# A planned attention and token/channel mixing kernel: transposes and loads expected to land later, and a larger stock of channel work

## The chip, the cores and the metric

One core of a Trainium2 chip. The time is the device time of one execution in microseconds (us). Most comparisons are of several timed runs of a kernel against runs of the kernel before on the same chip in the same rounds; a ratio is the mean time of one kernel's fast runs over the mean of the other's fast runs of those rounds, so it is not quite the ratio of the medians that stand beside it. A run counts as slow when it lies over 1.5% above the fastest of its kernel. On one core that is only a mark of length, and one of the findings below is what makes such runs long.

## The reference

Batch 8, 12 heads, sequence 448, head size 64. Attention without softmax, then a token mixer and a channel mixer:

```python
scores = q @ k.T / sqrt(64);  attn = maximum(scores, 0)**2 / 448;  x = attn @ v     # heads merged: [8, 448, 768]
h = maximum(x.T @ w_tok1, 0) @ w_tok2;  u = x + h.T                                 # w_tok1 [448, 256], w_tok2 [256, 448]
out = u + maximum(u @ w_ch1, 0) @ w_ch2                                             # w_ch1 [768, 1536], w_ch2 [1536, 768]
```

## The kernel before

The work is cut into 24 groups of four heads (three groups make a batch). Per group: 7 scores `S`, values `V`, a crossbar transpose of the attention output `xd` (from group 6 on), two token steps `t1` and `t2`. Per batch: 12 first channel steps `C1` and six or eight second ones `C2` (14 for a pair of batches). Keys and queries are transposed by TensorE up to group 8 and by a crossbar transfer `kd` from group 9 on, which reads from one interleave buffer `kqi` that VectorE or ScalarE fills.

Nothing of this runs in the order of the source. A planner in the kernel's own Python plays the program through with assumed durations and decides in which order each engine gets its instructions. On the chip that order is fixed; each engine waits at the head of its list (in the profile of before VectorE stood 4.17 us at one copy, and the scores behind it waited 1.60 us for its next eviction).

```python
class Planner:
    def run(self, todo, reserve, least, lanes=8):
        ...
                if o.work is not None:                       # a DMA: when does the planner expect it to land?
                    ring = max(ring, t + o.dur + 1.2) + o.work
                    o.seen = ring + 1.0 + SEM
                    landed[e].append(o.seen)
        ...
                    # o is attention work (scores, values): how much channel work is owed before the next?
                        over = sum(v for k, v in rest.items() if k < b) - reserve[min(b, len(reserve) - 1)]
                        owed += max(least, over / n)
...
    RES, LEAST = (0.0, 18.0, 10.0), 0.4
...
            xback[s] = add(Op(f"xd{s}", "SP", <crossbar transpose x_sb <- xT>, xe[s] + [old], dur=1.23, work=2.0))
            ready = xback[s]                                 # t1 waits for it
```

`rest` is the channel work of batches whose attention is done. What lies above `reserve` is spread between the attention work; what lies below is kept in hand, as filler for when attention has to wait.

## Time and profile before

| | before |
|---|---|
| timed runs first seen | 383.7 us median of 3 (383.02 to 388.58) |
| profiled execution | 382.1 us, span 380.2 |
| TensorE (PE) busy | 358.9 us of the span |
| TensorE idle: start, 40 to 280 us, tail | 5.1, 11.5, 4.7 us |
| crossbar transposes of x: landing min, median, max | 3.0, 6.0, 10.4 us |

In the profile's tables of stretches, the first figure after the stretch is its length, the next the time in which TensorE was busy, then weight loads, VectorE, ScalarE and GpSimd, the granted TensorE clock, the DMA share and GB/s. A line `A <- B: x, n, y` in the waits says that A waited for B x us in total, n times, y at the longest. The chain that ended last, by engine, of the kernel before:

```profile
PE 74%; DMA 17%; DVE 3%; ACT 3%; issue 2%; POOL 0%; ACTq 0%; DVEq 0%; POOLq 0%
```

17% of the path that set the end was spent in DMA: that is the share to watch.

### The profile page before, as it was taken

Reading aid. Unit: us, or ns where it says so; the run is one execution under the profiler, and the core shown is the slowest. Engines: PE = TensorE matmul, PEld = TensorE weight load, DVE = VectorE, ACT = ScalarE, POOL = GpSimd, SP = SyncE. Lnnn points to the kernel's source line nnn. Section 1 sums busy time; section 2 is a strip of 40 time slices with the busy share of each in tenths; the row PEclk is TensorE's granted clock in tenths of the full one; section 3 lists DMA queues with packets and bytes.
Section 4 is the critical chain, followed back from the end, with each engine's and each line's share of the span. In section 5 each row is a group of like instructions: output and inputs, shape, how many; then the busy total and the mean of one; then the engine's idle time right before and its main releaser. Section 6 shows DMA issues by size and latency. Waiting matters only on the chain.

```text
span 380.2 us, 8633 instructions
## 1 busy us (share of the span) xinstructions
PE 358.9 (94%) x3441; PEld 193.5 (51%) x3441; DVE 221.1 (58%) x406; ACT 210.5 (55%) x431; POOL 93.2 (25%) x159
## 2 busy tenths in 40 slices
PE   7998999999989999996998979999899999999995
PEld 3454555655455554543554534555446555565562
DVE  2999548764647774774265764568455785432021
ACT  3999858357646686265444465635662567512400
POOL 8992152840303330240033032031210000000000
PEclk9999999999999999999999998999999999999999
DMA  7999999999699999599199996996944641234023
GB/s 97 181 184 164 182 207 198 190 187 166 97 164 158 178 192 129 76 187 189 36 105 145 195 141 87 162 166 156 158 74 96 108 101 38 43 84 112 0 75 92
DMA packets 99352, 50.38 MB, mean 133 GB/s; under 512 B 72752, under 2 KB 95728, under 8 KB 99312
## 3 DMA queue, kind: packets, MB, share of 16 engines
q0 software_dynamic: 25424, 21.70, 42.8%
q1 hardware_dynamic: 73808, 27.93, 41.9%
q8 instruction: 27, 0.44, 0.5%
q14 instruction: 13, 0.11, 0.1%
q10 hardware_dynamic: 80, 0.20, 0.1%
HBM read 43.38 MB, written 11.01 MB: 143 GB/s over the span
## 4 chain that ended last, share of the span: by engine, by line
PE 74%; DMA 17%; DVE 3%; ACT 3%; issue 2%; POOL 0%; ACTq 0%; DVEq 0%; POOLq 0%
PE m_ps L762 24%; PE m_ps L729 23%; DMA x_sb<-xT 13%; PE acc_ps L538 8%; PE sc_ps L487 8%; PE t_ps L645 5%; PE h_ps L673 4%; DMA kqT<-kqi 3%; ACT sq L277 2%; DVE sq L520 1%; DMA q_raw<-in_q_dram 1%; PE kqT_ps L440 1%; ACT r_sb L277 1%; DVE kqT L285 0%; ACT kqT L283 0%
## 5 line engine op out<-in xcount | busy, mean ns | idle before, releaser
L277 ACT ACTIVATE sq<-sc_ps 128x448 bf16<-128x448 f32 x270 | 125.6, 571 | 40.0 <-PE sc_ps L487 40.0
L729 PE MATMUL m_ps<-uT_sb,wc 128*128 128x448 bf16 x576 | 116.2, 355 | 0.0
L762 PE MATMUL m_ps<-wc,r_sb 128*128 128x384 bf16 x672 | 114.1, 326 | 0.0
L520 DVE TENSOR_TENSOR sq<-sq 128x896 bf16<-128x896 bf16 x168 | 97.7, 618 | 6.4 <-ACT sq L277 6.2
L762 PEld LDWEIGHTS <-r_sb 128*128 128x128 bf16 x672 | 64.7, 98 | 45.3 <-issue 3.9
L729 PEld LDWEIGHTS <-wc 128*128 128x128 bf16 x576 | 55.4, 98 | 53.6 <-issue 5.8
L277 ACT ACTIVATE r_sb<-m_ps 128x448 bf16<-128x448 f32 x95 | 52.7, 556 | 48.4 <-PE m_ps L729 48.1
L300 POOL DMA_DIRECT2D v_raw<-in_v_dram x48 | 28.9, 611 | 169.6 <-PE sc_ps L487 159.2
L775 DVE TENSOR_TENSOR out_sb<-m_ps,u_sb 128x384 f32<-128x384 f32 x56 | 31.1, 556 | 61.1 <-PE m_ps L762 61.1
L279 DVE TENSOR_SCALAR sq<-sc_ps 128x448 bf16<-128x448 f32 x66 | 39.4, 619 | 43.6 <-PE sc_ps L487 43.6
L487 PE MATMUL sc_ps<-kqT 64*64 64x448 bf16 x672 | 52.9, 372 | 3.8 <-DVE out_sb L775 1.6
L538 PE MATMUL acc_ps<-sq,v_raw 64*64 64x448 bf16 x672 | 37.3, 356 | 0.0
L685 DVE TENSOR_TENSOR uT_sb<-h_ps,xT 128x448 bf16<-128x448 f32 x48 | 27.6, 617 | 12.7 <-PE h_ps L673 12.7
L645 PE MATMUL t_ps<-x_sb,wt 128*128 128x256 bf16 x192 | 25.7, 278 | 9.0 <-DMA x_sb<-xT 8.3
L487 PEld LDWEIGHTS <-kqT 64*64 64x64 bf16 x672 | 18.9, 107 | 28.5 <-issue 21.5
L277 ACT ACTIVATE r_sb<-t_ps 128x512 bf16<-128x512 f32 x24 | 14.8, 616 | 30.6 <-PE t_ps L645 30.3
L300 POOL DMA_DIRECT2D q_raw<-in_q_dram x48 | 29.4, 633 | 5.7 <-DMA wc<-in_moe_w_ch_dram 2.5
L300 POOL DMA_DIRECT2D k_raw<-in_k_dram x48 | 29.2, 623 | 2.6 <-PE sc_ps L487 0.9
L538 PEld LDWEIGHTS <-v_raw 64*64 64x64 bf16 x672 | 19.3, 108 | 15.1 <-issue 4.5
L645 PEld LDWEIGHTS <-wt 128*128 128x128 bf16 x192 | 17.8, 99 | 17.8 <-DMA x_sb<-xT 11.3
L566 DVE TENSOR_SCALAR xT<-acc_ps 128x448 bf16<-128x448 f32 x24 | 14.9, 621 | 16.9 <-PE acc_ps L538 16.9
L673 PE MATMUL h_ps<-wt,r_sb 128*128 128x448 bf16 x96 | 22.2, 354 | 1.7 <-ACT r_sb L277 1.5
(31 smaller groups left out, 99.3 us busy)
## 6 DMA issues: line engine op xcount, KB each, us to landing
out_dram<-out_sb SPq DMA_DIRECT2D x55, 192.0 KB, 3.3
k_raw<-in_k_dram POOLq DMA_DIRECT2D x48, 112.0 KB, 5.8
q_raw<-in_q_dram POOLq DMA_DIRECT2D x48, 112.0 KB, 6.5
v_raw<-in_v_dram POOLq DMA_DIRECT2D x48, 112.0 KB, 4.5
wc<-in_moe_w_ch_dram POOLq DMA_DIRECT2D x6, 768.0 KB, 13.5
u_sb<-uT_sb SPq DMA_TRANSPOSE x48, 4.8
x_sb<-xT SPq DMA_TRANSPOSE x18, 6.0
kqT<-kqi SPq DMA_TRANSPOSE x15, 5.6
```

The source lines that it names most:

```text
L277: nc.scalar.activation(out, ps, AF.Relu)
L279: nc.vector.tensor_scalar(out=out, in0=ps, scalar1=0.0, scalar2=None, op0=ALU.max)
L300: nc.gpsimd.dma_start(out=raws[t][s % NR][64 * half : 64 * (half + 1)], in_=src[b, h0 : h0 + 2].rearrange("e (p c) d -> p e (c d)", c=KC),)
L487: nc.tensor.matmul(o.ps[e][64 * half : 64 * (half + 1), :S], lhsT=kT[rows, half, c, :], rhs=qT[rows, half, :, :], start=True, stop=True, s ...
L520: lambda o: nc.vector.tensor_tensor(out=buf, in0=buf, in1=buf, op=ALU.mult),
L538: nc.tensor.matmul(o.ps[half][64 * e : 64 * (e + 1), :S], lhsT=r[rows, e, c * D : (c + 1) * D], rhs=sq[rows, e, :], start=(c == 0), stop=( ...
L645: nc.tensor.matmul(o.ps[:, j, :], lhsT=wt1[:, c, j * 128 : (j + 1) * 128], rhs=x_sb[:, :, c, :], start=(c == 0), stop=(c == 3),)
L673: nc.tensor.matmul(o.ps[:, :S], lhsT=r1[:, j, a * 128 : (a + 1) * 128], rhs=wt2[:, j, :], start=(j == 0), stop=(j == JC - 1),)
L685: nc.vector.tensor_tensor(out=uTs[bb % 2][:, 2 * i + a, off : off + S].rearrange("n (c p) -> n c p", c=KC), in0=t2.ps[:, :S].rearrange("n ...
L729: nc.tensor.matmul(o.ps[:, :S], lhsT=wc1[:, g, e * 128 : (e + 1) * 128], rhs=uT[:, g, off : off + S], start=(g == 0), stop=(g == CC - 1),)
L762: nc.tensor.matmul(o.ps[:, :HN], lhsT=r2[:, e, t * 128 : (t + 1) * 128], rhs=wc2[:, e, cols], start=(e == 0), stop=(e == EC - 1),)
L775: nc.vector.tensor_tensor(out=out_sb[:, cols].rearrange("n (g d) -> n g d", d=128), in0=u.ps[:, :HN].rearrange("n (g d) -> n g d", d=128), ...
```

## The change

The planner is told that what the sync queue issues (crossbar transposes, and stores) lands 5 us later than it thought, loads 1 us later, and it keeps more channel work in hand.

```diff
+LATE, LATE_IN = 5.0, 1.0
-                    o.seen = ring + 1.0 + SEM
+                    o.seen = ring + 1.0 + SEM + (LATE if e == "SP" else LATE_IN)
-    RES, LEAST = (0.0, 18.0, 10.0), 0.4
+    RES, LEAST = (0.0, 25.0, 20.0), 0.4
```

## The prediction

> **What bounds the kernel now.** I read, in this order: the busy row and the slices of the page, the table of busy time by stretch, the waits of TensorE, the landing times of the transposes, the chain of waits around the worst stall, and VectorE's timeline around another.
>
> ```profile
> PE 358.9 (94%) x3441; PEld 193.5 (51%) x3441; DVE 221.1 (58%) x406; ACT 210.5 (55%) x431; POOL 93.2 (25%) x159
> ...
> PE   7998999999989999996998979999899999999995
> ```
>
> TensorE (PE) is the bound: 358.9 of 380.2 us busy, no other engine over 58%. What a reordering can win is its 21.3 us of idle time, so the question is where they lie. The rows below (stretch, its length, PE busy, ...) tell it.
>
> ```profile
> 100.00:120.00 20.00, 18.95 (x154) 10.59 (x152) 11.54 (x22) 11.94 (x23) 6.78 (x12) 1.00 1.06 151
> ...
> 160.00:180.00 20.00, 16.53 (x145) 8.55 (x144) 13.15 (x24) 12.19 (x27) 6.13 (x11) 1.00 1.24 188
> ...
> 200.00:220.00 20.00, 18.08 (x176) 9.46 (x174) 13.32 (x25) 9.37 (x20) 4.41 (x8) 1.00 1.06 170
> 220.00:240.00 20.00, 16.81 (x122) 8.52 (x122) 9.87 (x19) 12.36 (x26) 6.30 (x11) 0.91 1.00 109
> ...
> 260.00:280.00 20.00, 18.49 (x175) 9.51 (x174) 12.93 (x24) 12.03 (x26) 4.42 (x8) 1.00 0.91 134
> ...
> 360.00:380.20 20.20, 15.48 (x96) 9.10 (x93) 4.46 (x8) 0.46 (x1) 0.00 (x0) 0.98 0.30 79
> ```
>
> Length less busy: 1.05 + 3.47 + 1.92 + 3.19 + 1.51, and 0.11 in 140 to 160, make 11.25 us of stalls between 100 and 280 us. The other 10 us are the start (5.1 us before 40 us, from the same table), 0.2 at 60 to 80 us and the tail (4.7 us: last eviction and stores). Who causes the 11.25:
>
> ```profile
> PE t_ps L645 <- DMA x_sb<-xT: 8.3, 5, 3.2
> PE sc_ps L487 <- DVE out_sb L775: 1.6, 1, 1.6
> ...
> PE sc_ps L487 <- DVE uT_sb L685: 0.8, 1, 0.8
> ```
>
> (waiter, releaser, us in total, times, longest). Five times the first token matmul stood for the crossbar transpose of its attention output: 8.3 us, three quarters of the stalls. The two waits of scores for VectorE have another origin: scores wait for a PSUM bank, and VectorE was itself standing, at the copy that fills the only interleave buffer, for a key/query transpose:
>
> ```profile
> 203.84 0.62 DVE L285 COPY kqi<-k_raw 128x896 bf16<-128x896 bf16 x1 [4.17 <-DMA kqT<-kqi]
> ...
> 205.51 0.57 PE L487 MATMUL sc_ps<-kqT 64*64 64x448 bf16 x7 [1.60 <-DVE out_sb L775]
> ```
>
> And the worst stall did more than stand. In the chain (start, us, what) the 8.76 us transpose is followed by a token group of 1.71 us, elsewhere 1.05 after a stall, and a channel group of six of 2.15 us, elsewhere 1.13, while the granted clock in that stretch is 0.91: about 0.66 + 1.02 = 1.7 us more.
>
> ```profile
> 220.10 8.76 DMA x_sb<-xT
> 228.90 1.71 PE t_ps L645 x8
> 230.61 2.15 PE m_ps L729 x6
> ```
>
> So what is there to win in the stretch that the change can touch is 11.25 + 1.7 = 13 us, 3.4% of 383.7.
>
> [...] the load queue holds 42.8% and the transpose and store queue 41.9% of the 16 engines' span, and the same x transpose lands after 3.0 us at best, 6.0 in the middle, 10.4 at worst; the late groups, issued when no load is left, are the fast ones. [...]
>
> **The change, part by part.** No instruction is added or removed; both instruction lists have 6884 PE rows. Only the order moves, and the order is static: a planner's pessimism costs nothing by itself on the chip, where each engine runs its list as soon as it can.
>
> (1) Transposes are expected 5 us later. By the constants in the code the planner put an x transpose at 1.23 + 1.2 + 2.0 + 1.06 = 5.5 us from issue, below the measured median of 6.0, so more than half of the groups are planned too early. With 5 more it is 10.5, which is just the measured worst (10.4). For the key/query transpose it goes from 6.7 to 11.7, over the measured worst of 10.5.
>
> To see whether the new order really covers it, I counted the PE work that stands between the end of the value matmuls of a group and its first token matmul in both orders, with the durations from the chain: scores 0.25 (0.50 for two), values 1.40, a channel group 1.135 (six) or 1.95 (twelve), token 0.87 and 0.38. Example, group 15, the worst stall. Before: 5 scores, two second-token halves and 4 first-channel groups, 1.25 + 0.76 + 4.54 = 6.5 us. Needed: 1.23 us from the values' end to the issue (eviction) and 8.76 to land = 10.0. Short by 3.5; the trace shows 3.19. So the count works. After: 8 scores, two token halves, 4 second-channel groups and the values of group 16, 2.0 + 0.76 + 7.8 + 1.4 = 12.0 us. Covered by 2.
>
> For all 18 groups (6 to 23) the cover is 6.5 to 10.5 us before and 11.2 to 15.1 after. The need in the trace is 0.8 to 1.3 us to the issue (once 3.4, behind four stores) plus landing. Its five largest are 11.5, 11.0, 10.7, 10.0 and 8.4 us (groups 7, 12, 14, 15, 18), and the new cover of these is 15.1, 13.8, 11.2, 12.0 and 15.0. All are held; the margin is thin only at groups 13, 14, 19, 22 and 23 (11.2 to 11.9), of which the last two run when landings take 3 us. Gain: all of 8.3 us.
>
> (2) The copies into the interleave buffer sit later in the lists of VectorE and ScalarE, after evictions that used to stand behind them. The blocked copies (4.17 us once, 5.1 us in all) should shrink below a microsecond. Gain: 1.6 + 0.8 of score waits and 0.4 of a second-token wait, 2.8 us. Key/query transposes are not exposed otherwise: each lands 17 us or more before its first score.
>
> (3) The stock of channel work (reserves 25 and 20 instead of 18 and 10) is what supplies the filler for (1). The new order shows it: between a batch's last token group and its first channel group lie 8 to 15 us of other work from batch 1 on, where before it was 0.5 to 4.3 us in all batches but one. Alone it wins nothing.
>
> (4) Loads expected 1 us later: the load queue's list is the same row for row, and PE waits for loads only 0.5 us in all. Nothing.
>
> (5) The slow clock after the 3.19 us stall goes with the stall: 1.7 us.
>
> (6) Switches between half-array and full-array work cost PE 283 ns start to start instead of 189, 0.09 us each. The old order has 115 and the new 109: 0.5 us.
>
> Untouched: the first 102 PE groups stand in the same order, so the start (5.1 us) stays; the tail (4.7 us) ends in the same second-channel groups.
>
> Sum: 8.3 + 2.8 + 1.7 + 0.5 = 13.3 at most. I take off 2 us for new stalls (below): 11.3, so 383.7 - 11.3 = 372.4 us, 2.9% less.
>
> **The rivals.** First, landings grow as the order tightens. In the stretches where loads run the DMA share is already 1.0 to 1.3, and every group's loads are issued by the very event, the end of its values, that lets its x transpose go; attention now ends some 10 us of PE work earlier, so 3% more traffic per time. For it: landing follows load, as said above. Against: cover rises by 4 to 7 us and this would have to eat it all. At thin groups it may cost 1 to 2 us; that is the 2 us above. If landings grew to 14 us, half of the gain would be gone: 378.
>
> Second, a new block at the head of a list: out-stores too are now expected 5 us later, and with three output rows the planner may place output evictions late in VectorE's list, so that PSUM banks stay full and PE waits for VectorE. For it: VectorE's list is the most changed. Against: 58% busy, eight banks, and its waits for second-channel matmuls (61.1 us) show it standing ready. At 1 us in each of the last 6 half-batches: 378.
>
> Third, PE was behind its plan anyway and the stalls were luck of one profiled run, so that an average run has less to win. Against: the three timed runs (383.0, 383.7, 388.6) are not shorter than the profiled one (382.1); the scatter upward is what exposed landings would make.
>
> **Range and chances.** Full gain with the start unchanged: 370. Half of it: 377. Range 369 to 378. Faster by 2% means below 376, which needs 7.7 of the 13.3 us: 0.80. Within 2%: 0.18. Slower by 2% would need a new block of 20 us: 0.02.
>
> **What would show it.** Right: PE's wait for x_sb falls from 8.3 to below 1.5 us, PE busy in the stretches from 100 to 280 us above 19.7 of 20, no granted clock below 1.00 there, landing of x still 3 to 11 us, VectorE's wait at the interleave copy below 1 us, span near 369. Wrong on (1): waits for x_sb stay while landings pass 12 us. Wrong on the second rival: a new row, scores or channel matmuls waiting for VectorE, of several us. A longer start or tail would mean that I misread what the change leaves alone.

## The result, and the profile after

| | before | after |
|---|---|---|
| timed runs, same rounds | 384.68 us median of 4 (383.02 to 388.58) | 366.86 us median of 4 (364.96 to 369.94) |
| ratio of the fast runs | | 0.953, 95% interval 0.943 to 0.963 |
| profiled execution | 382.1, span 380.2 | 365.9, span 364.0 |

Faster by 4.7%, where 2.9% was forecast; 366.9 lies below the range of 369 to 378. The page of the changed kernel, its busy row, its slices of TensorE and of the granted clock, and its chain:

```profile
PE 354.0 (97%) x3441; PEld 193.0 (53%) x3441; DVE 227.2 (62%) x415; ACT 205.0 (56%) x422; POOL 93.1 (26%) x159
...
PE   7998999999999999999999999999999999999994
...
PEclk9999999999999999999999999999999999999998
...
PE 91%; DVE 3%; ACT 2%; issue 1%; DMA 1%; POOL 1%; ACTq 0%; POOLq 0%
```

The slices have no hole between the start and the tail, the clock none before the tail, and DMA has fallen from 17% of the chain to 1%. The stretches that held the stalls before, and the last one:

```profile
160.00:180.00 20.00, 20.00 (x158) 11.08 (x157) 10.20 (x20) 8.00 (x18) 3.57 (x6) 1.00 0.99 164
...
220.00:240.00 20.00, 20.00 (x187) 10.73 (x185) 12.61 (x23) 15.91 (x34) 6.06 (x11) 1.00 1.03 158
...
340.00:364.00 24.00, 19.35 (x116) 11.15 (x114) 4.45 (x8) 2.18 (x4) 0.00 (x0) 0.96 0.26 67
```

TensorE is busy 20.00 of 20 us from 80 us to the tail of 4.65 us. All waits of TensorE that are left, all of them before 70 us:

```profile
PE warm_ps L362 <- DVE wt L359: 1.5, 1, 1.5
PE sc_ps L488 <- ACT kqT L284: 1.2, 2, 0.6
PE h_ps L674 <- ACT r_sb L278: 1.1, 2, 0.6
PE kqT_ps L441 <- DMA q_raw<-in_q_dram: 0.5, 2, 0.3
PE t_ps L646 <- ACT sq L278: 0.5, 1, 0.5
```

The wait for `x_sb` is gone. The transposes are no faster for it; the landing times of `x_sb` in the changed kernel:

```profile
DMA to landing us min/median/max: 3.2/5.8/12.9
```

The spans differ by 16.2 us. 11.3 of it is idle time of TensorE (380.2 - 358.9 = 21.3 before, 364.0 - 354.0 = 10.0 after). The other 4.9 is busy time. I took from both traces the time from the start of each matmul to the start of the next, and set it against the median for that pair of kinds. Three terms come out: the slow clock after the 3.19 us stall (granted 0.50 from 229.1 to 232.5 us), 1.7 us; some 2.5 us in which matmuls that had been delayed still count as busy, because a matmul's modelled end lies some 0.17 us after the next could start (a first channel matmul counts as busy for 0.35 us and the next starts after 0.19), so that a stall shows as that much too short and the shortest ones not at all; and 0.7 us of pairs that are cheaper in the new order, most of it the six switches saved.

### The profile page after: what moved, and what is told of

It reads as the page before. It is cut to its first block, busy times and chain, and to the rows that moved or that the text cites. A ratio compares the mean times of both kernels' runs of the same rounds, so it can differ in the third digit from the quotient of the medians.

```text
span 364.0 us, 8631 instructions
## 1 busy us (share of the span) xinstructions
PE 354.0 (97%) x3441; PEld 193.0 (53%) x3441; DVE 227.2 (62%) x415; ACT 205.0 (56%) x422; POOL 93.1 (26%) x159
## 4 chain that ended last, share of the span: by engine, by line
PE 91%; DVE 3%; ACT 2%; issue 1%; DMA 1%; POOL 1%; ACTq 0%; POOLq 0%
PE m_ps L763 30%; PE m_ps L730 30%; PE sc_ps L488 10%; PE acc_ps L539 9%; PE t_ps L646 6%; PE h_ps L674 5%; DVE sq L521 1%; ACT sq L278 1%; DMA q_raw<-in_q_dram 1%; PE kqT_ps L441 1%; DVE kqT L286 0%; ACT kqT L284 0%; DVE x_sb L286 0%; ACT r_sb L278 0%; POOL k_raw L301 0%
## 5 line engine op out<-in xcount | busy, mean ns | idle before, releaser
L278 ACT ACTIVATE sq<-sc_ps 128x448 bf16<-128x448 f32 x262 | 121.9, 570 | 35.3 <-PE sc_ps L488 35.3
L280 DVE TENSOR_SCALAR sq<-sc_ps 128x448 bf16<-128x448 f32 x74 | 44.2, 619 | 29.8 <-PE sc_ps L488 29.7
L488 PE MATMUL sc_ps<-kqT 64*64 64x448 bf16 x672 | 51.4, 372 | 1.3 <-ACT kqT L284 1.2
L567 DVE TENSOR_SCALAR xT<-acc_ps 128x448 bf16<-128x448 f32 x24 | 14.9, 620 | 9.9 <-PE acc_ps L539 9.9
```

What stands on the lines that cost most here:

```text
L278: nc.scalar.activation(out, ps, AF.Relu)
L280: nc.vector.tensor_scalar(out=out, in0=ps, scalar1=0.0, scalar2=None, op0=ALU.max)
L488: nc.tensor.matmul(o.ps[e][64 * half : 64 * (half + 1), :S], lhsT=kT[rows, half, c, :], rhs=qT[rows, half, :, :], start=True, stop=True, s ...
```

## The experiments

Sixteen runs were made (e13 and e14 are the kernel before, e15 the changed one). Times are medians of all runs, ratios are of the fast ones; by the record's 2% rule the changed kernel, e3 and e4 are faster, e1, e2, e8 and e11 the same, and the others unclear, so I go by the intervals. "Stock" is the reserves, "late" the lateness, 5 us in the changed kernel.

| run | what it is | median us (n, range) | ratio, 95% interval |
|---|---|---|---|
| changed kernel | late 5, stock 25/20 | 366.86 (4, 364.96 to 369.94) | 0.953 (0.943 to 0.963) |
| e1 | late 0, stock 25/20 | 379.64 (4, 378.25 to 384.79) | 0.988 (0.981 to 0.995) |
| e2 | late 5, stock 18/10 | 383.13 (12, 382.36 to 384.35) | 0.999 (0.996 to 1.002) |
| e3 | late for x alone, stock 25/20 | 371.01 (4, 367.26 to 373.35) | 0.960 (0.951 to 0.970) |
| e4 | old order, loads cut | 369.67 (4, 369.03 to 374.33) | 0.966 (0.957 to 0.975) |
| e5 | late 2, stock 25/20 | 370.21 (4, 368.52 to 376.3) | 0.961 (0.950 to 0.972) |
| e6 | late 4, stock 25/20 | 366.58 (4, 365.63 to 368.62) | 0.954 (0.945 to 0.963) |
| e7 | late 8, stock 25/20 | 383.18 (4, 378.19 to 385.91) | 0.989 (0.972 to 1.007) |
| e8 | e2 with squares cut | 382.15 (20, 381.2 to 384.05) | 1.001 (0.999 to 1.003) |
| e9 | e2 with ScalarE's ReLUs cut | 383.34 (12, 382.36 to 385.79) | 1.007 (1.003 to 1.012) |
| e10 | changed kernel with ScalarE's ReLUs cut | 366.11 (4, 365.58 to 371.87) | 0.956 (0.943 to 0.969) |
| e11 | e2 with ReLUs and squares cut | 377.46 (20, 373.36 to 381.9) | 0.986 (0.983 to 0.990) |
| e12 | late 6, stock 30/25 | 368.16 (4, 367.21 to 372.24) | 0.966 (0.958 to 0.975) |
| e16 | changed kernel, group 9 on TensorE | 367.0 (6, 366.44 to 367.37) | 0.955 (0.950 to 0.961) |

e13 to e15 are single profiled runs and stand below. My theory was that only one sum matters: the TensorE work between a group's values and its first token step (the cover) against the eviction plus the landing (the need). The rivals were that the stock is the gain itself, and that the key/query side is.

### One half of the change at a time: e1, e2, e3

```diff
 e1: LATE, LATE_IN = 0.0, 0.0      RES = (0.0, 25.0, 20.0)
 e2: LATE, LATE_IN = 5.0, 1.0      RES = (0.0, 18.0, 10.0)
 e3: (LATE if e == "SP" and o.name[:2] == "xd" else 0.0 if e == "SP" else LATE_IN)     RES = (0.0, 25.0, 20.0)
```

> The larger stock alone (reserves 25 and 20, both lateness terms zero). Counted with measured durations, the PE work between a group's values and its first token matmul is 6.7 to 12.7 us here, much as before (6.5 to 10.5), and 6.7 to 8.8 in all groups from 12 on. Theory A (cover against landing is all that matters): stalls for x_sb remain, 5 to 12 us in total, and the time stays within 1.5% of before, 380 to 386 us. Rival B (the stock, by moving channel work later, is itself the gain): under 374 us.

Measured 379.6, just below the 380 that I gave as its edge. In its profile (of a slow run) the wait that the change was to remove is as large as ever:

```profile
PE t_ps L646 <- DMA x_sb<-xT: 11.6, 6, 3.9
```

A stock that the planner sees no reason to spend does not help at the right moment. It gains 1.2% by the ratio, which I did not trace further.

> Later landings (5 and 1 us) with the old stock (18 and 10). Counted cover is 11 to 21 us up to group 17, but 8.3, 6.4, 6.9, 7.1 at groups 18 to 21 and zero work between some first and second token matmuls, since channel work has run out. Theory A: most of the gain comes, but one to three waits return late in attention (x_sb under 3 us in total, token evictions 1 to 3 us); 368 to 373 us. Rival B (the stock is the gain): above 378.

This missed by 10 us, and taught most. The wait for `x_sb` is 0.4 us, as the theory says, and yet the time is that of before. One row of waits has grown, that of second token steps for their ReLU, which is 1.1 us in the changed kernel:

```profile
PE h_ps L674 <- ACT r_sb L278: 5.7, 7, 1.2
```

The larger part of the loss stands in no row of waits. The stretch from 280 to 300 us in the late-only kernel e2:

```profile
280.00:300.00 20.00, 18.55 (x206) 8.68 (x204) 18.95 (x36) 16.45 (x38) 4.76 (x8) 1.00 0.88 159
```

and in the changed kernel:

```profile
280.00:300.00 20.00, 20.00 (x182) 11.57 (x174) 15.35 (x29) 8.54 (x19) 0.00 (x0) 1.00 0.50 104
```

VectorE at 18.95 and ScalarE at 16.45 of 20 us are the engines that evict scores. The order list shows why: with the small stock the channel work is spent by 285 us (the planner put 12 first channel steps in a row shortly before), and then up to 24 scores follow each other without a channel step between them, 4 at most in the changed kernel. TensorE's timeline in e2 (start, us, what):

```profile
292.07 4.49 PE L488 MATMUL sc_ps<-kqT 64*64 64x448 bf16 x28
```

28 matmuls are 7 scores. The four of one score start within some 10 ns of each other and the next score 0.19 us later when nothing waits; here one to four matmuls start every 0.43 us, and a score takes 0.4 to 0.9 us. That is so for 25 of the 85 scores of e2 that directly follow another after 40 us, and for 3 of 77 in the changed kernel. Since a matmul counts as busy for 0.37 us, TensorE looks all but busy while it goes at less than half its pace. Adding up the time from each matmul's start to the next one's, and booking it to the latter, e2's profile is 18.3 us longer than the changed kernel's: 8.2 on the way to scores, 5.1 to second token steps, 2.4 to values, the rest to others. Busy time does not show the loss: e2's page has PE at 363.4 us, 95% of the span, more than the 358.9 us of before.

> The new stock, but 5 us later only for the x transposes; key/query transposes, u transposes and stores as before. Cover 11.3 to 17.0. If the key/query part (copies into the interleave buffer blocking VectorE) matters, 1 to 3 us of waits of scores for VectorE stay and the time is 368 to 371. If the x part is all, within 0.7% of the changed kernel, 364 to 369.

Measured 371.0, in the range of the first branch, but not by its wait: no score waited for VectorE at the copy. The profile has a 2.0 us wait for `x_sb` (group 6, landing after 15.7 us) and 1.7 us of scores waiting for the transfer of group 9 itself. Its interval overlaps that of the changed kernel, so the key/query part is worth a few us at most.

### Why the transposes land late: e4

```diff
 in load(), for groups s >= 8 (wrong result on purpose):
-    out=raws[t][s % NR][64 * half : 64 * (half + 1)],          in_=src[...]
+    out=raws[t][s % NR][64 * half : 64 * (half + 1), :1, :D],  in_=src[...][:, :1, :D]
```

> The kernel before in its own order, but the key, query and value loads of groups 8 and up fetch one fourteenth of their bytes (wrong result on purpose). If the x transposes land late because they share the DMA engines with loads, they land after 3 to 5 us throughout, all waits for x_sb go without any reordering, and the time is 367 to 373. If they wait on their own queue (u transposes, stores), landings stay at 5 to 10 us and the time above 378.

Measured 369.7, with the order of before untouched. The landings of `x_sb` in e4:

```profile
DMA to landing us min/median/max: 3.0/3.9/5.8
```

No wait for `x_sb` is left, and the landings of before were 3.0, 6.0 and 10.4 us. So it is the bytes of the loads that made the transposes late (the load queue's share of the 16 DMA engines fell from 42.8% to 23.3%, with as many loads issued), and the old order would have been good enough for unhindered ones. (Its profiled run has one 3.6 us wait of another kind, for the channel weights near 48 us, so e4 undersells itself a little.)

### How late is late enough: e5, e6, e7, e12

```diff
 e5: LATE = 2.0   e6: LATE = 4.0   e7: LATE = 8.0     RES = (0.0, 25.0, 20.0)
 e12: LATE = 6.0                                      RES = (0.0, 30.0, 25.0)
```

> New stock, lateness 2 us instead of 5. Counted cover of the x transposes 8.5 to 14.5 us (changed kernel 11.2 to 15.1, before 6.5 to 10.5). Needs seen in the changed kernel were 11 to 14 at groups 6, 7 and 16, 9.5 at 9 and 10, under 7 in most others. Theory (cover against need): one to three stalls for x_sb, 1 to 4 us in total; 367 to 373 us. If any lateness at all had been enough, equal to the changed kernel, 364 to 368.

> New stock, lateness 4. Cover 10.6 to 17.0, and 107 switches between half-array and full-array work instead of 109. Theory: no stall or one under 2 us, 364 to 369, within 0.7% of the changed kernel.

> New stock, lateness 8. The planner runs out of channel work: up to 10 scores in a row without channel work between (4 in the changed kernel, 24 in the late-only one), no work between some first and second token matmuls, 127 switches (1.6 us more), cover only 5.6 to 9.1 at four groups. Theory (stock and lateness must match): 369 to 377, lost as token waits for ReLU and as scores at the pace of the evictions, not as waits for x_sb. If more lateness is only safer: 364 to 368.

> Lateness 6 with reserves 30 and 25: stock raised along with lateness. Cover 13.1 to 17.2 us, at most 4 scores in a row without channel work, 123 switches against 109 (1.3 us). If stock and lateness must match, no stalls come back, unlike lateness 8 with 25 and 20: 365 to 370. If lateness over 5 is bad by itself: above 373.

e5 came as the count said: 370.2, with a wait of 1.8 us at group 10 and one of 1.1 at group 6, where landings of 9.9 and 12.9 us met too little cover. e6 has one wait of 0.9 us and is as fast as the changed kernel. e7 lost nearly everything, more than I gave it: 383.2. The wait for `x_sb` is 0.5 us there; token steps waiting for their ReLU, scores for the key/query transfer and for VectorE have come in its place, and a granted clock of 0.91 in the stretch from 180 to 200 us:

```profile
PE h_ps L674 <- ACT r_sb L278: 4.0, 5, 1.1
PE sc_ps L488 <- DMA kqT<-kqi: 3.2, 2, 2.4
PE sc_ps L488 <- DVE sq L280: 1.9, 2, 0.9
```

e12 fits the idea that lateness needs stock: at 6 us, with the stock raised too, no wait stands in the part of the program where the orders differ, and the time is 368.2. That more stock would have saved 8 us of lateness, or that 6 us would have failed without it, is not shown; neither was run.

### What paces a row of scores: e8 to e11

```diff
 e8:  e2 and  tensor_tensor(out=buf[:, :, :56], in0=buf[:, :, :56], in1=buf[:, :, :56])           # squares
 e9:  e2 and, for s >= 7, on ScalarE only:  relu(o, buf[:, e, :112], u.ps[e][:, :112])
 e10: the changed kernel and the same ReLUs as e9
 e11: e2 and, for s >= 7, ReLUs on both engines and squares on 112 columns        (all wrong results on purpose)
```

> The late-only kernel (old stock) with the squares cut to an eighth of their columns (wrong result on purpose), same order. Its scores advanced 0.43 us per two matmuls where 0.19 is the matmuls' own pace. If the pace of the runs of scores is set by the evictions (per score two ReLUs of 0.57 to 0.62 and one square of 0.62 over two engines: 1.8 / 2 = 0.9 us per four matmuls), the advance falls to about 0.33 and the time by 3 to 6 us from the late-only 383, to 377 to 380. If the loss is elsewhere (TensorE clock, DMA), less than 1.5 us.

> The late-only kernel (old stock), same lists, but ScalarE's ReLUs of scores from group 7 on handle a quarter of their columns (wrong result on purpose). The cheap squares changed nothing: ScalarE stood in an unbroken row of ReLUs, 13 in 5.78 us, two per score, 0.87 us per score where the matmuls take 0.38. If ScalarE's list is the pace of the runs of scores, their advance of 0.43 us per two matmuls falls to about 0.2 to 0.3, the token waits for ScalarE (5.7 us) shrink too, and the time falls by 7 to 13 us to 370 to 376. If not, within 1.5 us of 383.

> Control: the same cheaper ReLUs in the changed kernel. There TensorE stands for nothing between 40 us and the tail, so nothing on ScalarE is exposed: within 0.5% of the changed kernel, 364 to 369 us.

> The late-only kernel, same lists, with the score ReLUs on both engines and the squares cut to a quarter of their columns from group 7 on (wrong result on purpose). Cheaper squares alone left ScalarE as the pace, cheaper ReLUs on ScalarE alone made VectorE the pace (15 operations in a row). If the runs of scores go at the pace of the evictions as a whole, only this one frees them: advance near 0.19 us per two matmuls, 7 to 11 us off, 371 to 377; the token waits for their own ReLU (4 us) stay. If it stays within 1.5 us of 383, the late-only kernel's loss is not in the evictions and I have no theory for it.

These texts set 0.43 beside 0.19 us, both as the advance of two matmuls. The traces bear out the first: the ReLUs in a row start 0.43 us apart, each frees the bank of two of a score's four matmuls, and a score with both ReLUs on ScalarE takes 0.87 us. The second was a misreading: 0.19 us is the advance of a whole score. So the 0.38 us per score should be 0.19, and the rows are slower against TensorE's own pace than the texts have it.

e8 and e9 both missed, 382.2 and 383.3 where I expected 377 to 380 and 370 to 376. The lists are fixed, so relief on one engine does not move its work to the other. In e2, ScalarE's timeline is one row of ReLUs:

```profile
287.26 5.78 ACT L278 ACTIVATE sq<-sc_ps 128x448 bf16<-128x448 f32 x13 [0.88 <-PE sc_ps L488]
```

Cutting VectorE's squares (e8) leaves that row as it is. Cutting ScalarE's ReLUs (e9) leaves VectorE's list, and now scores wait for it, with the idle time in the brackets:

```profile
287.33 1.29 PE L488 MATMUL sc_ps<-kqT 64*64 64x448 bf16 x15 [0.20 <-DVE sq L280]
...
290.53 0.76 PE L488 MATMUL sc_ps<-kqT 64*64 64x448 bf16 x12 [0.54 <-DVE sq L280]
292.67 0.96 PE L488 MATMUL sc_ps<-kqT 64*64 64x448 bf16 x12 [1.38 <-DVE xT L567]
295.32 0.58 PE L488 MATMUL sc_ps<-kqT 64*64 64x448 bf16 x3 [1.69 <-DVE sq L280]
```

The granted clock was lower too: e9's page has it between 0.8 and 0.9 in the slices from 210 to 220 and from 287 to 306 us, where e2's stretches show 1.00, so e9's time does not tell what cheaper ReLUs alone are worth. Only relief on both (e11) lets the scores run: 32 matmuls, eight scores, in

```profile
283.54 1.98 PE L488 MATMUL sc_ps<-kqT 64*64 64x448 bf16 x32
```

and the time falls to 377.5 (fastest run 373.4, profiled span 372.7), just past the upper edge of what I expected; by the ratios, from 0.999 to 0.986, some 5 of the 16 us. So the evictions as a whole pace a row of scores: added up in the same way, the way to scores is 1.6 us longer than in the changed kernel, where it was 8.2 in e2. What e11 does not win back is other waits. Second token steps still come 3.4 us later (they wait 4.0 us for their ReLU), and first ones 2.5 us, with a new wait for `x_sb` of 2.1 us: two transposes landed after 13.4 and 14.6 us; what made them that late was not shown. Why the timed runs lie above the profiled one (374.6) is not on record. The control e10, 366.1 us, is the changed kernel within its scatter: there no eviction is exposed.

### Why the gain was larger than the profile of before allowed: e13, e14

The same kernel before, profiled twice more.

> The kernel before, profiled once more. If its scatter is made of exposed landings, TensorE's idle time between 40 us and its last matmul plus the slow-clock excess varies from run to run (13.5 us in the first profile) and span less that excess stays the same, about 380.2 - 13.5 = 367 us within 1.5. If the scatter has another source, the excess is equal and the span differs.

> The same as e13, a third profile: span less stalls and slow-clock excess again 367 within 1.5 us.

The runs took 391.3 and 387.8 us, spans 389.4 and 385.9. The waits for `x_sb` in e13:

```profile
PE t_ps L645 <- DMA x_sb<-xT: 11.3, 5, 5.4
PE sc_ps L487 <- DVE uT_sb L685: 3.5, 1, 3.5
```

and the stretch around group 15, the worst stall again:

```profile
220.00:240.00 20.00, 14.63 (x100) 7.28 (x99) 6.50 (x12) 7.03 (x15) 3.57 (x6) 0.76 0.97 111
```

5.37 us of that stretch TensorE stood, and the granted clock, over the whole stretch, was 0.76: six first channel matmuls after the stall took 2.20 us, against 1.30 at full clock. Adding up, as above, what pairs of matmuls took beyond their median (pairs over by 0.06 us or more, after 40 us) gives 15.2 us in the first profile, 25.3 in e13 and 20.0 in e14. Span less this excess is 365.0, 364.1 and 365.9: spans that differ by 9.2 us agree within 1.8. (My 367 came from 13.5 instead of 15.2; the part of a stall that counts as busy was missing.) In these three profiles the scatter of before is made of exposed landings, delays behind them and the slow clock that follows, and the profile that I predicted from was one of its short runs.

### What scatter is left: e15, e16

> The changed kernel, profiled again: x transposes all land in time (no wait for x_sb over 0.5 us), 364 to 370; if over 367, then by a wait of scores for the key/query transpose of group 9 near 100 us.

> The changed kernel with group 9's keys and queries transposed by TensorE as groups 0 to 8 are, so that the first key/query transfer has a later deadline. Costs 0.6 us of TensorE work. If the thin margin of group 9 is what scatters the changed kernel, the runs close up (365 to 368) and the median stays within 0.5% of 366.9; if not, they still spread to 370.

```diff
 e16: the changed kernel with
-    XDMA, TDMA = 6, 9
+    XDMA, TDMA = 6, 10
```

e15 took 368.1 us. Contrary to what I wrote, an x transpose was late too, that of group 6; its waits of TensorE that the first profile lacked:

```profile
PE t_ps L646 <- DMA x_sb<-xT: 1.7, 1, 1.7
...
PE sc_ps L488 <- DMA kqT<-kqi: 1.2, 1, 1.2
```

Group 9's key/query transfer, issued at 85.2 us, landed after 18.6 us, and group 6's x transpose, issued before it, after 15.5. In the changed kernel's first profile the same two took 11.1 and 12.9 us and were in time by 4.1 and 0.8 us. The control e10 had 4.1 us of waiting at group 9 in its profiled run of 371.9 us. e16, which takes that first key/query transfer away, closes the runs up to 366.44 to 367.37 us, six of them within 0.3%, with no wait for either. The median is the same; on these six runs, all on one chip, it is the steadier kernel.

## Why the prediction was right or wrong

- What bounds the kernel: right. TensorE was the bound, its holes were the prize, and nothing but order moved.
- Step (1), the cover: right. Group 15's cover came out as 11.8 us in the changed kernel (12.0 counted), all 18 groups as 11.1 to 14.9 (11.2 to 15.1 counted), and the 8.3 us went. (The list's 6884 PE rows are 6882 in the trace: 3441 matmuls and as many weight loads.) e4 shows the need from the other side, e5 and e6 the dose.
- Step (2), the blocked copies: the waits of scores went, 2.8 us with them. They went in e3 too, where key/query transposes are not expected later, so that part of the change is not what removed them. That each key/query transfer lands 17 us before its first score was true of before alone. The new order spent that margin: 4 to 16 us in the changed kernel, and group 9's is the one that fails at times.
- Step (3), the stock: "alone it wins nothing" was near (e1, 0.988), but I treated it as an aid to (1). It is a condition: without it (e2), or with too much lateness for it (e7), the gain is lost, in e2 to scores at the pace of their evictions and to second token steps waiting for their ReLU. e11 bears out the first; e12, at 6 us, fits but does not prove it for e7.
- Step (4), loads: the load queue's list is the same and no loads were waited for after the start. The 1 us was not tried alone.
- Step (5), the slow clock: 1.7 us in the trace, as predicted. In the changed kernel the granted clock is 1.00 from 100 to 355 us.
- Step (6), switches: 0.5 to 0.6 us as said, in an order that is 0.7 us cheaper in all.
- The size is what failed, in three terms of the sum. The allowance of 2 us for new stalls was not needed in most runs. The removable time in that one profile was 16 us, not 13.3: stalls read as idle time leave out the part hidden under modelled ends, 2.5 us, and the order is 0.2 us cheaper than counted. And I set the gain of a short profiled run (382.1) against the median (383.7). These are 2.0, 2.7 and 1.6 us; less the 0.9 us by which the changed kernel's median lies above its profiled run, they make 5.4 of the 5.5 us between 372.4 and 366.9. The third rival looked at just this and drew the wrong conclusion from it. That upward scatter "is what exposed landings would make" means that the mean run had more to win (e13: 25.3 us of excess against 15.2), so the top of the range was safe and the bottom was not.
- The first rival, landings that grow, came true in one place: 12.9 us at group 6 in the first profile, inside a cover of 14.5, and 15.5 in e15, outside it by 1.7. The second, output evictions in the way, did not show.

## What to carry to other kernels

In a statically ordered program a wait is paid for by the work that stands between the issue and the use, so count that work against the worst landing in the trace, not the median, and count what the kernel's slower runs show as well. Room for latency needs filler: widening one without the other moved much of the loss here into a form that neither idle time nor a row of waits shows, a pipelined engine that looks busy at less than half its pace (in e2 a score took 0.4 to 0.9 us where 0.19 is its pace). Look at start-to-start times, and at the engines that evict.

## What else the traces show

- The slow clock after a stall, in four waits for `x_sb`. In the first profile of before, after 3.19 us the granted clock was 0.50 from 229.1 to 232.5 us, and six first channel matmuls took 2.36 us; after 2.23 us it stayed at 1.00, and six took 1.30. In e13, after 5.37 us, six took 2.20. In e14 a wait of 2.20 us was followed within 1.5 us by six that took 2.45 us, 0.37 us from start to start where 0.19 is usual (its page has the clock between 0.8 and 0.9 in the slice from 174 to 183 us). So the length of a wait alone does not sort these four; what does was not shown.
- The landing time of an x transpose (128 x 1024 bf16, SBUF to SBUF) depends on the traffic beside it. In the first profile of before the four issued after the last load landed after 3.0 to 4.4 us, the fourteen others after 4.1 to 10.4, with the median of all at 6.0. With the loads cut it was 3.0 to 5.8 us (e4); beside loads it was up to 15.5 (e15) and 15.7 us (e3).
- What the reordering is worth includes scatter: the kernel before scattered from 378 to 395 us over all its timed runs, and the steadiest reordered one (e16) from 366.4 to 367.4, in far fewer runs.
